# mLSTM attention and a top-1 mixture of experts in one kernel: list scatters without mutual waits, the last two items routed together, the first expert as 256 + 256 rows

## The chip, the cores and the metric

The kernel runs on one core of a Trainium2 chip. The metric is the device time of one launch in microseconds; lower is better. The numbers of the profile come from one execution that the hardware profiler recorded, the numbers of the runs from separate executions without it.

## The reference

An mLSTM recurrence over 4 batches, 8 heads, 768 tokens and a head width of 40 gives rows of 320 values for 3072 tokens; a mixture of 8 experts with top-1 routing follows. Cut to what matters:

```python
for t in range(S):                                   # per batch and head
    m_new = np.maximum(f_gate[:, :, t] + m, i_gate[:, :, t])
    f_stab, i_stab = np.exp(f_gate[:, :, t] + m - m_new), np.exp(i_gate[:, :, t] - m_new)
    C = f_stab * C + i_stab * np.einsum('bhd,bhe->bhde', vt, kt)
    n = f_stab * n + i_stab * kt
    denom = np.maximum(np.abs(nq), 1.0)              # nq = n . q
    y[:, :, t] = sigmoid(o_gate) * (C @ qt) / denom
x = y.transpose(0, 2, 1, 3).reshape(3072, 320)
logits = x @ w_gate
expert_idx = np.argmax(logits, axis=1)
gate_w = softmax(logits)[np.arange(N), expert_idx]
for e in range(8):
    xe = x[expert_idx == e]
    out[expert_idx == e] = gate_w * (np.maximum(xe @ w1[e], 0) @ w2[e])   # w1 320x1024, w2 1024x320
```

All is fp32. The experts' products run as fp32r in three parts each: an operand is split into a high part and a low part (its rest), and high x high, high x low and low x high are added.

## The kernel before

**Attention.** The recurrence is computed in chunks of 128 tokens: 6 chunks x 4 batches make 24 items (`NITEM`), taken one after the other. Step s of the loop does the score products of item s (`scores`, PE L282, DVE L292), the value products of item s-1 (`attend`, PE L309, DVE L326, then L346, which also gives the routing logits) and the end of item s-2 (`finish`, L350 to L368: the divisor, the output rows `xs`, the logits `lg`). A decay mask `dd` for each item is made by ACT and cut by GpSimd (L254); GpSimd also scales queries (`qg`, L269) and keys (`kw`, L272). PE reads `qbd` (queries by head), DMA brings it; `gb` is the item's gate row for `qg`. The finished rows go to `x_dram` (`store`, L371).

**Routing.** Groups of items (`GROUPS`: four times 4, three times 2, then item 22 and item 23 alone) go through `choose` (L377 to L395: maximum, one-hot `oh`, running counts `ohs`), `weights_of` (L399, an exponential on ACT), `count` (L401, three small matmuls for the places) and `place` (L409 to L424: the gate weight into `rec`, the place in the expert's list into `slot`, last the CAST L424). `scatter(it)` (L426) is an indirect DMA, issued by GpSimd, that writes the 128 records of an item to their places in `lst` in DRAM; one or two scatters are issued in each step. All scatters write the same DRAM tensor.

**Experts.** Expert 0 in order of size, called the first, takes its tokens of items 0 to 17 (at most HEAD = 384) as unit "a", and its late ones as unit "b" of 128 rows. A unit is read by `load_list` (L503, the list's rows by SP) and `gather` (L506, an indirect DMA for each tile of 128 rows, GpSimd), transposed on PE by thirds (`third`: L526, ACT L527, DVE L529), multiplied by w1 in eight slices f (`first`: PE L541 8 matmuls a slice, ACT L550 `hh`, DVE L551 `hl`) and by w2 for each tile of 128 rows j (`second`: PE L564 24 matmuls a tile, ACT L568, scattered to the output L569). `first` runs a few slices ahead of the hh and hl of its own slices, and calls a function in each slice; for unit a this is `last(f)`, which holds the routing of items 22 and 23. After unit a's `second` come unit b's thirds (inside the last tile), `first` and `second` of b, and then expert 1 with four tiles, 512 rows.

**Weights.** An expert's weights come in 7 chunks (`fetch`, `pull`: w1 in three of 512 KB, w2 in four of 320 KB, four raw buffers) on SP's queue; each chunk is split by ACT (high, L499) and DVE (low, L500) in `split`. The first expert's chunks are loaded in steps 14 to 20; three are split in the steps of `SPLITS`, 16, 18 and 20, (L739 and L765), the other four in slices 2, 3, 5 and 7 of unit a's `first`.

**Order.** The body is written out by hand under a manual schedule: each engine's instructions stand in the order of the code, and the framework adds the waits that the data need. On SP the loads, stores, list reads and weights share one queue in that order.

## Time and profile before

| | |
|---|---|
| Runs | 449.1, 445.7 and 447.39 us; median 447.39 us |
| Span of the profiled execution | 448.4 us |
| PE (matmul) busy | 388.3 us, 87% |
| DVE busy | 264.6 us, 59% |
| ACT busy | 195.1 us, 44% |
| GpSimd (POOL) busy | 153.4 us, 34% |
| Read from and written to DRAM | 57.97 and 8.78 MB |

PE is the engine with the most work, but the span has stretches of different kinds: attention fills it up to about 206 us, the first expert runs from 206.04 to 255.89 us, and the others after that. A busy share over the whole span says little about one stretch, so the rows below are of short windows and of single instructions. In the rows of a timeline the start, the duration, the engine, the line and operation, output and input stand in that order, and in brackets the idle time of that engine ahead of the instruction and what ended it. PE is busy while a matmul is in flight, and two overlap, so the price of one matmul is the distance between two starts and not its duration.

### The profile page before, as it was taken

The page shows a single profiled execution, that of the slowest core. Times are in us where ns is not written, and L with a number is a line of the kernel's source. Part 1 is how long each engine was busy: PE and PEld are TensorE (multiplying, and loading weights), DVE is VectorE, ACT ScalarE, POOL GpSimd, SP SyncE. Part 2 cuts the span into 40 slices and gives each one's busy share as a digit, 9 for nine tenths or more (in the row PEclk, how much of TensorE's full clock was granted, in tenths as well). Part 3 has the DMA queues.
Part 4 walks back from the last instruction along what each step waited for, and adds up shares of the span by engine and source line. Part 5 has one row for each costly group of instructions (what it writes and reads, how often), then busy time and mean ns, then how long its engine had stood idle before and what let it go on. Part 6 is the DMA issues. An engine that isn't in the chain of part 4 may idle for free. (4 is left out here: it accounts for less than half of the span.)

```text
span 448.4 us, 7609 instructions
## 1 busy us (share of the span) xinstructions
PE 388.3 (87%) x2489; PEld 350.2 (78%) x2489; DVE 264.6 (59%) x737; ACT 195.1 (44%) x438; POOL 153.4 (34%) x166
## 2 busy tenths in 40 slices
PE   7868969969968859669959999999999999979970
PEld 3657858859856738459959989889999999979970
DVE  6477978968958848478823254384572737364300
ACT  3747545526357254102623245263353646454310
POOL 5433536555643443362161031321402222221020
PEclk8989998989989879979975699999999999999995
DMA  8987685887988788521483335435445464651000
GB/s 192 235 203 188 191 213 144 190 205 178 199 217 216 183 213 186 148 69 36 95 238 103 112 103 165 118 110 168 131 146 160 109 205 131 198 157 33 12 22 11
DMA packets 42572, 66.47 MB, mean 148 GB/s; under 512 B 9232, under 2 KB 30876, under 8 KB 42516
## 3 DMA queue, kind: packets, MB, share of 16 engines
q1 hardware_dynamic: 38668, 57.35, 49.7%
q0 software_dynamic: 3456, 8.36, 6.0%
q8 instruction: 20, 0.33, 0.3%
q10 hardware_dynamic: 408, 0.27, 0.3%
q14 instruction: 20, 0.16, 0.1%
HBM read 57.97 MB, written 8.78 MB: 149 GB/s over the span
## 5 line engine op out<-in xcount | busy, mean ns | idle before, releaser
L282 PE MATMUL bank<-qbd,tq 120*128 120x384 f32 x144 | 58.6, 553 | 30.2 <-DMA qbd<-in_qk 22.1
L564 PE MATMUL bank<-w2h,hh 128*128 128x320 f32 (+1 forms) x224 | 71.8, 321 | 0.0
L551 DVE SCALAR_TENSOR_TENSOR hl<-bank,hh 128x384 fp32r<-128x384 f32 (+4 forms) x72 | 39.4, 550 | 52.3 <-ACT hh L550 51.8
L564 PE MATMUL bank<-w2l,hh 128*128 128x320 f32 (+1 forms) x224 | 70.1, 313 | 0.0
L564 PE MATMUL bank<-w2h,hl 128*128 128x320 f32 (+1 forms) x224 | 70.1, 313 | 0.0
L282 PEld LDWEIGHTS bank<-qbd,tq 120*128 120x128 f32 x144 | 30.5, 226 | 49.6 <-issue 16.3
L541 PE MATMUL bank<-xh,w1h 128*128 128x384 f32 (+3 forms) x192 | 67.2, 352 | 0.0
L541 PE MATMUL bank<-xh,w1l 128*128 128x384 f32 (+3 forms) x192 | 67.0, 350 | 0.0
L569 POOL DMA_INDIRECT out<-y,ls x24 | 23.6, 982 | 120.1 <-ACT y L568 113.2
L250 ACT ACTIVATE dd<-bank,aT 128x128 f32<-128x128 f32 x192 | 52.1, 382 | 20.2 <-PE bank L238 13.4
L292 DVE TENSOR_TENSOR pp<-bank,dd 128x384 f32<-128x384 f32 (+1 forms) x72 | 34.1, 508 | 39.5 <-PE bank L282 28.8
L550 ACT ACTIVATE hh<-bank 128x384 fp32r<-128x384 f32 (+4 forms) x72 | 35.1, 488 | 51.2 <-PE bank L541 49.3
L309 PE MATMUL bank<-pp,vz 128*123 128x128 f32 x384 | 53.1, 274 | 0.0
L309 PEld LDWEIGHTS bank<-pp,vz 128*123 128x123 f32 x384 | 47.6, 187 | 0.0
L541 PE MATMUL bank<-xl,w1h 128*128 128x384 f32 (+3 forms) x128 | 44.7, 350 | 0.0
L564 PEld LDWEIGHTS bank<-w2h,hh 128*128 128x128 f32 (+1 forms) x224 | 42.0, 188 | 0.0
L564 PEld LDWEIGHTS bank<-w2l,hh 128*128 128x128 f32 (+1 forms) x224 | 41.9, 187 | 0.0
L564 PEld LDWEIGHTS bank<-w2h,hl 128*128 128x128 f32 (+1 forms) x224 | 41.8, 187 | 0.0
L427 POOL DMA_INDIRECT lst<-rec,slot x24 | 25.0, 1043 | 43.2 <-DMA lst<-rec,slot 23.0
L269 POOL TENSOR_TENSOR qg<-tq,gb 120x384 f32<-120x384 f32 x20 | 21.2, 1059 | 53.2 <-DMA gb<-g_dram 26.8
L541 PEld LDWEIGHTS bank<-xh,w1h 128*128 128x128 f32 x192 | 36.1, 188 | 2.8 <-DVE hl L551 0.2
L541 PEld LDWEIGHTS bank<-xh,w1l 128*128 128x128 f32 x192 | 36.1, 188 | 2.5
(164 smaller groups left out, 690.7 us busy)
## 6 DMA issues: line engine op xcount, KB each, us to landing
raw<-in_w SPq DMA_DIRECT2D x32, 320.0 KB
tq<-in_qk SPq DMA_DIRECT2D x24, 360.0 KB
tk<-in_kv SPq DMA_DIRECT2D x24, 344.5 KB
raw<-in_w SPq DMA_DIRECT2D x16, 512.0 KB
sg<-in_og SPq DMA_DIRECT2D x6, 720.0 KB
raw<-in_w SPq DMA_DIRECT2D x16, 256.0 KB
x_dram<-xs SPq DMA_DIRECT2D x24, 160.0 KB
gb<-g_dram SPq DMA_DIRECT2D x20, 180.0 KB
```

Of the source, the lines that this page charges most:

```text
L250: nc.scalar.activation(dd[:, h, :], bc_ps[h // 4][:, h % 4], AF.Exp, bias=aT[:, c, i : i + 1], scale=-1.0)
L269: nc.gpsimd.tensor_mul(qg, t["tq"][:, 1], t["gb"])
L282: nc.tensor.matmul(s_ps[g][:, : n * P].rearrange("p (j t) -> p j t", j=n), t["tq"][:, 0, g, :], qbd[it % 3][:, g, :n, :], start=True, stop ...
L292: nc.vector.tensor_mul(_of(pp, g), s_ps[g][:, : n * P].rearrange("p (j t) -> p j t", j=n), _of(t["dd"], g))
L309: nc.tensor.matmul(hT, vz[it % 3][:, g, j * HW_ : (j + 1) * HW_], t["pp"][:, NG * j + g, :], start=(c == 0 and j == 0), stop=(j == n - 1),)
L427: nc.gpsimd.indirect_dma_start(out=lst, out_offset=bass.IndirectOffsetOnAxis(ap=slot[:, it : it + 1], axis=0), in_=rec[:, it, :], in_offse ...
L541: nc.tensor.matmul(ph[:, :n], a[:, k, fs], b[:, k, :n], start=not last and i == 0, stop=last and i == 2)
L550: nc.scalar.activation(hh[:, f, :n], ph[f][:, :n], AF.Relu)
L551: nc.vector.scalar_tensor_tensor(hl[:, f, :n], ph[f][:, :n], 0.0, f32(hh[:, f, :n]), ALU.max, ALU.subtract)
L564: nc.tensor.matmul(py[:T], a[:, f, ts], b[:, f], start=(f == 0 and i == 0), stop=(f == NF - 1 and i == 2))
L569: nc.gpsimd.indirect_dma_start(out=out, out_offset=bass.IndirectOffsetOnAxis(ap=ls[:T, j, 1:2].bitcast(I32), axis=0), in_=y[:T], in_offset ...
```

## The change

1. **Scatters.** They are declared to have no dependence among each other (their rows are disjoint); a one-element `memset` of a `spacer` tile precedes each. `load_list` gets a dependence on every scatter so far.
2. **Items 22 and 23** are one group of two. `finish(23)` comes ahead of unit a's `first`, with the logits ahead of the rows; the gate weights (`share`) are made in slice 0, the places, both scatters and the reads of unit b's list in slice 2.
3. **The first expert** is 256 rows in unit a (`HT` = 2 tiles) and 256 rows in unit b.
4. **Weights.** All 7 chunks of the first expert are split in steps 16 to 22 of attention. The register of expert 1 is read, and its first four chunks (512, 512, 512 and 320 KB) are loaded, at the end of the last step; its splits take the places that the first expert's had in unit a's `first`, and two tiles and three slices after. The registers of experts 2 to 7 are read after unit b's list.
5. **Start.** Of nine 512-column matmuls on zeros two stay; 24 small fp32 ones on tiles of the array follow.

```diff
-HEAD = 3 * P
+HT = 2
+HEAD = HT * P
-    i0 + n - 1: (i0, n) for i0, n in ((0, 4), (4, 4), (8, 4), (12, 4), (16, 2), (18, 2), (20, 2), (22, 1), (23, 1))
+    i0 + n - 1: (i0, n) for i0, n in ((0, 4), (4, 4), (8, 4), (12, 4), (16, 2), (18, 2), (20, 2), (22, 2))
...
-    def finish(it):
+    def finish(it, late=False):
...
+        if not late:
+            yield rows()
...
         yield nc.vector.tensor_reduce(lg[:, it, :], pl.rearrange("p g j e -> p e (g j)"), axis=AX.X, op=ALU.add)
+        if late:
+            yield rows()
...
+    scattered = []
+
     def scatter(it):
-        nc.gpsimd.indirect_dma_start(
+        nc.gpsimd.memset(spacer, 0.0)
+        ins = nc.gpsimd.indirect_dma_start(
             out=lst, out_offset=bass.IndirectOffsetOnAxis(ap=slot[:, it : it + 1], axis=0),
             in_=rec[:, it, :], in_offset=None,
         )
+        for other in scattered:
+            tc.declare_no_dep(ins.ins, other.ins, reason="disjoint rows")
+        scattered.append(ins)
...
     def load_list(ls, row, J, T):
-        nc.sync.dma_start(ls[:T, :J], lst[ds(row, T * J)].rearrange("(p j) w -> p j w", j=J))
+        ins = nc.sync.dma_start(ls[:T, :J], lst[ds(row, T * J)].rearrange("(p j) w -> p j w", j=J))
+        landed = mybir.DependencyInfo(mybir.DependencyClass.Sync, mybir.DependencyReason.DATA)
+        for other in scattered:
+            tc.add_manual_dep(ins.ins, other.ins.name, landed, reason="every scatter so far has landed")
...
+    def stir_tiles():
+        z = busy.bitcast(F32)
+        for a in (0, 64) * 4:
+            nc.tensor.matmul(bank[a // 64][:, :P], z[a : a + D, :P], z[a : a + D, :P], start=True, stop=True)
+        for a in (0, 64) * 4:
+            nc.tensor.matmul(bank[2][a : a + D + 1, :P], z[:, : D + 1], z[:, :P], start=True, stop=True)
...
-        stir(9)
+        stir(2)
+        stir_tiles()
...
-    SPLITS = (FIRST + 4, FIRST + 6, FIRST + 8)
+    SPLITS = range(FIRST + 4, NITEM - 1)
...
-            load_list(ls0, es[0] * SS, 3, P)
+            load_list(ls0, es[0] * SS, HT, P)
...
-            if chunks:
+            if s == NITEM:
+                expert(1)
+                sets[1] = {}
+                fetch(es[1], sets[1])
+                pull()
+            elif chunks:
                 pull(1)
...
         third(2)
-        weave(choose(NITEM - 2, 1))
-        weights_of(NITEM - 2, 1)
         store(NITEM - 2)
-        for r in range(1, E):
-            expert(r)
-        fetch(es[1], sets[1])
-        pull()
+        weave(finish(NITEM - 1, late=True))
+        weave(choose(NITEM - 2, 2))
+        weights_of(NITEM - 2, 2)
+        store(NITEM - 1)
         xs = {}
 
         def last(f):
             if f == 0:
-                weave(finish(NITEM - 1))
-                store(NITEM - 1)
-            if f == 1:
-                count(NITEM - 2, 1)
-                weave(place(NITEM - 2, 1), choose(NITEM - 1, 1))
+                weave(share(NITEM - 2, 2))
+            if f == 2:
+                count(NITEM - 2, 2)
+                weave(place(NITEM - 2, 2))
                 scatter(NITEM - 2)
-                weights_of(NITEM - 1, 1)
-            if f == 4:
-                count(NITEM - 1, 1)
-                weave(place(NITEM - 1, 1))
                 scatter(NITEM - 1)
-                xs["b"] = take("b", es[0] * SS + HEAD, 1, P)
+                xs["b"] = take("b", es[0] * SS + HEAD, 4 - HT, P)
+                for r in range(2, E):
+                    expert(r)
                 xs[1] = take(1, es[1] * SS, *CAPS[1])
-            if f in (2, 3, 5, 7):
+            if f in (5, 7):
                 split()
 
         first("a", sets[0], xh0, xl0, HEAD, last)
-        xt, third = transpose_x("b", xs["b"][1], 1, P)
+        xt, third = transpose_x("b", xs["b"][1], 4 - HT, P)
...
-        second("a", sets[0], ls0, 3, P, lambda j: split(), ahead)
+        second("a", sets[0], ls0, HT, P, lambda j: split(), ahead)
...
         def inner(f):
-            if f % 2:
+            if f in (1, 3, 5):
                 split()
-            if f in (1, 3, 5):
                 third1(f // 2)
```

Three places show how the instructions stand now. The first is GpSimd at the end of attention, before: `dd`, `qg` and the last scatters of attention up to the gathers of unit a (the waits in brackets are semaphores; DMASW ones are of GpSimd's own transfers, Pool of its own earlier instructions).

```order
L427 DMA lst<-rec,slot 28672x3 [waits DMASW5_49]
L254 AFFINE_SELECT dd_1910<-dd_1910 128x1024 [waits Activation_49]
L427 DMA lst<-rec,slot 28672x3 [waits DMASW6_49]
L269 TENSOR_TENSOR qg_1945<-tq_1750,gb_1840 120x384 [waits DMAHW0_49,DMAHW1_49,PE_49,Pool_49]
L427 DMA lst<-rec,slot 28672x3 [waits DMASW7_49,DVE_49]
L254 AFFINE_SELECT dd_2007<-dd_2007 128x1024 [waits Activation_49]
L427 DMA lst<-rec,slot 28672x3 [waits DMASW0_49]
L269 TENSOR_TENSOR qg_2034<-tq_1842,gb_1930 120x384 [waits DMAHW0_49,DMAHW1_49,PE_49,Pool_49]
L254 AFFINE_SELECT dd_2086<-dd_2086 128x1024 [waits Activation_49]
L269 TENSOR_TENSOR qg_2108<-tq_1932,gb_2024 120x384 [waits DMAHW0_49,DMAHW1_49,PE_49,Pool_49]
L508 DMA xg_101<-x_dram,ls_100 128x320 [waits DMAHW4_49,DMAHW5_49,DMAHW3_49,DMAHW2_49]
L508 DMA xg_101<-x_dram,ls_100 128x320 x2
```

And in the changed kernel, where L443 and L444 are the memset and the scatter, L256 is the mask, L271 `qg` and L537 the gather.

```order
L444 DMA lst<-rec,slot 28672x3 [waits DMASW7_49]
L271 TENSOR_TENSOR qg_1983<-tq_1782,gb_1874 120x384 [waits DMAHW1_49,DMAHW0_49,PE_49]
L443 MEMSET spacer 1x1 [waits Pool_49]
L444 DMA lst<-rec,slot 28672x3 [waits DMASW0_49,DVE_49]
L256 AFFINE_SELECT dd_2046<-dd_2046 128x1024 [waits Activation_49]
L443 MEMSET spacer 1x1 [waits Pool_49]
L444 DMA lst<-rec,slot 28672x3 [waits DMASW1_49]
L271 TENSOR_TENSOR qg_2075<-tq_1876,gb_1968 120x384 [waits DMAHW1_49,DMAHW0_49,PE_49]
L256 AFFINE_SELECT dd_2128<-dd_2128 128x1024 [waits Activation_49]
L271 TENSOR_TENSOR qg_2151<-tq_1970,gb_2064 120x384 [waits DMAHW1_49,DMAHW0_49,PE_49]
L537 DMA xg_102<-x_dram,ls_101 128x320 [waits DMAHW4_49,DMAHW3_49,DMAHW5_49,DMAHW2_49,DMASW2_49]
L537 DMA xg_102<-x_dram,ls_101 128x320 [waits DMASW3_49]
```

The order of the work is the same. The waits of `qg` for earlier GpSimd work are gone, each scatter has a memset ahead of it, and a scatter waits for the one eight indirect transfers before, whose semaphore it takes, in place of the one just ahead.

The second is DVE in unit a's `first`, before, where item 23 is routed: L413 to L415 make the gate weight, L420 to L424 the place, with the first expert's splits (L500) and the low parts `hl` of slices around them.

```order
L500 TENSOR_TENSOR w2l_1388<-raw_1742,w2h_1387 128x640 [waits Activation_49]
L551 SCALAR_TENSOR_TENSOR hl<-bank_132,hh 128x384 [waits Activation_49]
L500 TENSOR_TENSOR w2l_1388<-raw_1834,w2h_1387 128x640 [waits Activation_49]
L551 SCALAR_TENSOR_TENSOR hl<-bank_133,hh 128x384 [waits Activation_49]
L413 TENSOR_REDUCE es_2451<-ex_2408 128x1
L414 TENSOR_SCALAR es_2451<-es_2451 128x1 [waits DVE_49]
L415 RECIPROCAL rec<-es_2451 128x1 [waits DVE_49]
L420 TENSOR_TENSOR sl_2455<-bank_137,bump 128x8 [waits PE_49]
L421 TENSOR_TENSOR sl_2455<-sl_2455,oh 128x8 [waits DVE_49]
L423 TENSOR_REDUCE ss_2458<-sl_2455 128x1 [waits DVE_49]
L424 CAST slot<-ss_2458 128x1 [waits DVE_49]
L551 SCALAR_TENSOR_TENSOR hl<-bank_134,hh 128x384 [waits Activation_49]
```

And in the changed kernel, from the end of `choose` for both items to the places of both.

```order
L403 TENSOR_TENSOR oh<-sc_2354,m_2356 128x16 [waits DVE_49]
L405 TENSOR_TENSOR ohs<-ohs,oh 128x8 [waits DVE_49] x2
L580 SCALAR_TENSOR_TENSOR hl<-bank_133,hh 128x256 [waits DMAHW5_49,DMAHW6_49,DMAHW2_49,DMAHW7_49,DMAHW0_49,Activation_49]
L422 TENSOR_REDUCE es_2379<-ex_2361 128x2
L423 TENSOR_SCALAR es_2379<-es_2379 128x2 [waits DVE_49]
L424 RECIPROCAL rec<-es_2379 128x2 [waits DVE_49]
L580 SCALAR_TENSOR_TENSOR hl<-bank_134,hh 128x256 [waits Activation_49]
L580 SCALAR_TENSOR_TENSOR hl<-bank_135,hh 128x256 [waits Activation_49]
L433 TENSOR_TENSOR sl_2401<-bank_138,bump 128x16 [waits PE_49]
L434 TENSOR_TENSOR sl_2401<-sl_2401,oh 128x16 [waits DVE_49]
L436 TENSOR_REDUCE ss_2404<-sl_2401 128x2 [waits DVE_49]
L437 CAST slot<-ss_2404 128x2 [waits DVE_49]
```

The places of both items (the CAST, L437) stand behind the third `hl`, and no split of weights is ahead of them; before, item 23's stood behind the sixth `hl` and two splits.

The third is SP behind attention, before: the last register reads, the store of item 23 (`xs_2373`), two chunks of expert 1 and the list of unit b.

```order
L464 ISA x2
L464 TENSOR_LOAD er
L464 ISA x2
L371 DMA x_dram<-xs_2373 128x320 [waits DMAHW6_49,DVE_49]
L493 ISA
L493 DMA raw_2422<-in_w 128x1024 [waits DMAHW7_49,DVE_49]
L493 ISA
L493 DMA raw_2436<-in_w 128x1024 [waits DMAHW0_49,DVE_49]
L504 ISA
L504 DMA lsb<-lst 128x3 [waits DMASW2_49,DMAHW1_49,PE_49,Pool_49]
```

And in the changed kernel, where the stores are those of items 22 and 23 and the weights are those of expert 1.

```order
L511 ISA
L511 DMA raw_2314<-in_w 128x1024 [waits DMAHW6_49,Activation_49]
L511 ISA
L511 DMA raw_2316<-in_w 64x1024 [waits DMAHW7_49,Activation_49]
L511 ISA
L511 DMA raw_2316<-in_w 64x1024 [waits DMAHW0_49]
L511 ISA
L511 DMA raw_2319<-in_w 128x2x320 [waits DMAHW1_49,Activation_49]
L381 DMA x_dram<-xs_2281 128x320 [waits DMAHW2_49,DVE_49]
L381 DMA x_dram<-xs_2345 128x320 [waits DMAHW3_49,DVE_49]
L530 ISA
L530 DMA lsb<-lst 128x6 [waits DMASW4_49,DMASW5_49,DMASW1_49,DMASW6_49,DMASW0_49,DMASW7_49,PE_49,DMAHW4_49,Activation_49,Pool_49]
```

The chunks of expert 1 stand ahead of the stores of items 22 and 23 now (four chunks, five transfers, of which the first is not in these rows), and the list of unit b has twice the rows and waits for more transfers.

## Rows read from the trace of the kernel before

**Rows 1.** The page's slices: the span in 40 slices of 11.2 us, the mean busy share of the DMA engines in tenths.

```profile
DMA  8987685887988788521483335435445464651000
```

**Rows 2.** Windows of core 0: the window and its length in us, busy time (and instructions) of PE, PE's weight loads, DVE, ACT and POOL, then the granted clock as a share of full speed, the DMA engines' busy share and GB/s.

```profile
180.00:190.00 10.00, 5.97 (x39) 4.64 (x39) 4.03 (x14) 1.27 (x5) 3.19 (x4) 0.96 0.53 149
190.00:200.00 10.00, 6.50 (x24) 4.87 (x24) 8.77 (x26) 0.00 (x0) 6.52 (x7) 0.70 0.15 38
240.00:250.00 10.00, 10.00 (x50) 9.89 (x49) 5.27 (x11) 3.63 (x10) 0.98 (x1) 0.50 0.38 121
```

**Rows 3.** Waits from 155 to 235 us, of PE and of POOL: who waited at which line, for what, then the total in us, the number of waits and the longest.

```profile
PE bank L282 <- DMA qbd<-in_qk: 5.4, 1, 5.4
PE bank L526 <- DMA xgb<-x_dram,lsb: 4.9, 1, 4.9
POOL lst L427 <- DMA lst<-rec,slot: 18.7, 6, 5.2
```

**Rows 4.** Timeline of POOL at the end of attention.

```profile
179.11 0.97 POOL L427 DMA_INDIRECT lst<-rec,slot  x1 [3.56 <-DMA lst<-rec,slot]
186.28 1.00 POOL L427 DMA_INDIRECT lst<-rec,slot  x1 [5.16 <-DMA lst<-rec,slot]
187.31 1.10 POOL L254 TENSOR_SCALAR_AFFINE_SELECT dd<-dd 128x1024 f32<-128x1024 f32 x1
190.44 0.97 POOL L427 DMA_INDIRECT lst<-rec,slot  x1 [2.03 <-DMA lst<-rec,slot]
192.39 1.09 POOL L254 TENSOR_SCALAR_AFFINE_SELECT dd<-dd 128x1024 f32<-128x1024 f32 x1
196.84 1.01 POOL L508 DMA_INDIRECT xg<-x_dram,ls  x1 [2.41 <-DMA ls<-lst]
```

**Rows 5.** Timeline of DVE and of PE in the same stretch: the masking of scores, and the two PE instructions behind the longest idle times.

```profile
188.44 1.35 DVE L292 TENSOR_TENSOR pp<-bank,dd 128x384 f32<-128x384 f32 x3 [5.79 <-POOL dd L254]
189.05 3.64 PE L282 MATMUL bank<-qbd,tq 120*128 120x384 f32 x6 [2.73 <-DVE pp L292]
196.20 1.84 PE L346 MATMUL bank<-cs,yT 123*128 123x147 f32 x6 [3.50 <-DVE yT L326]
```

**Rows 6.** Timeline of PE at the end of attention: six of unit a's nine transposes, and its first product.

```profile
205.46 0.82 PE L526 MATMUL bank<-cs,xg 128*128 128x128 f32 x6
206.04 0.42 PE L541 MATMUL bank<-xh,w1h 128*128 128x384 f32 x1
```

**Rows 7.** The chain of unit b: the places of items 22 and 23 (DVE), their scatters and the gather of unit b (POOL), the list's read (SP).

```profile
213.08 0.15 DVE L424 CAST slot<-ss 128x1 int32<-128x1 f32 x1
214.68 0.96 POOL L427 DMA_INDIRECT lst<-rec,slot  x1 [2.74 <-DVE w2l L500]
217.13 0.15 DVE L424 CAST slot<-ss 128x1 int32<-128x1 f32 x1
220.03 0.99 POOL L427 DMA_INDIRECT lst<-rec,slot  x1 [4.39 <-DVE hl L551]
223.42 0.33 SPq L504 DMA_DIRECT2D lsb<-lst  x1
226.81 0.98 POOL L508 DMA_INDIRECT xgb<-x_dram,lsb  x1 [5.79 <-issue]
```

**Rows 8.** Transfers by issue: from issue to landing in us, the least, the median and the most of all scatters (the source line L427), then the other gathers with their median, and the gather of unit b.

```profile
DMA to landing us min/median/max: 2.5/5.6/9.4
xg<-x_dram,ls POOLq DMA_INDIRECT x27, 2.9
xgb<-x_dram,lsb POOLq DMA_INDIRECT x1, 5.8
```

**Rows 9.** Timeline of GpSimd and DVE at 230 us: a gather's issue beside the low part of a weight chunk.

```profile
230.45 1.23 DVE L500 TENSOR_TENSOR w1l<-raw,w1h 128x1024 fp32r<-128x1024 f32 x1 [5.86 <-ACT w1h L499]
230.61 1.88 POOL L508 DMA_INDIRECT xg<-x_dram,ls  x1 [0.30 <-issue]
```

**Rows 10.** Timeline of PE: the first and the 66th product of unit a's second stage; then the start of unit b (transposes), two neighbouring 128-column products, the first product of its second stage, the product of that stage at which the distance of starts went from 0.25 to 0.14 us, and the start of expert 1.

```profile
218.02 0.31 PE L564 MATMUL bank<-w2h,hh 128*128 128x320 f32 x1
227.55 0.30 PE L564 MATMUL bank<-w2h,hl 128*128 128x320 f32 x1
232.75 0.87 PE L526 MATMUL bank<-cs,xgb 128*128 128x128 f32 x3 [4.89 <-DMA xgb<-x_dram,lsb]
235.34 0.41 PE L541 MATMUL bank<-xlb,w1h 128*128 128x128 f32 x1
235.55 0.41 PE L541 MATMUL bank<-xhb,w1l 128*128 128x128 f32 x1
250.84 0.57 PE L564 MATMUL bank<-w2h,hh 128*128 128x320 f32 x1
254.13 0.31 PE L564 MATMUL bank<-w2h,hh 128*128 128x320 f32 x1
255.89 0.40 PE L541 MATMUL bank<-xh,w1h 128*128 128x512 f32 x1
```

**Rows 11.** The window around unit b's gathers, in the columns of the other windows.

```profile
228.00:230.00 2.00, 0.00 (x0) 0.00 (x0) 0.00 (x0) 0.63 (x1) 1.60 (x2) 1.00 1.02 272
```

**Rows 12.** Timeline of PE at the start: the zeros' products and the second item's scores.

```profile
1.26 3.90 PE L636 MATMUL bank<-busy 128*128 128x512 bf16 x9 [1.26 <-DVE busy L643]
19.02 1.96 PE L282 MATMUL bank<-qbd,tq 120*128 120x384 f32 x6 [2.19 <-DMA qbd<-in_qk]
```

More of the change, by code (lines that the diff above doesn't have):

```diff
@@ L407, in count, with share @@
         nc.tensor.matmul(pos, ones, baseb[:, :n], start=False, stop=True)
-    def place(i0, n):
-        o3 = oh[:, i0 : i0 + n, :]
-        pos = rt.pop(("pos", i0))
+    def share(i0, n):
         es = sm.tile([P, n], F32, name=f"es{i0}", tag="es")
@@ L415, in place @@
         yield nc.vector.reciprocal(rec[:, i0 : i0 + n, 2], es)
+    def place(i0, n):
+        o3 = oh[:, i0 : i0 + n, :]
+        pos = rt.pop(("pos", i0))
         sl = sm.tile([P, n, E], F32, name=f"sl{i0}", tag="sl")
@@ L698, in routing @@
         i0, n = GROUPS[s - 3]
+        yield from share(i0, n)
         yield from place(i0, n)
@@ L738, in step @@
         if s in SPLITS:
-            nc.scalar.copy(loaded[0][1], loaded[0][0])
+            high(loaded[0])
         if ok(s + 1):
@@ L763, in step @@
         if s in SPLITS:
-            t, h, l = loaded.pop(0)
-            nc.vector.tensor_sub(l, t, f32(h))
+            low(loaded.pop(0))
         if s == 2:
@@ L798, in step @@
         if s == EARLY + 4:
-            gather(xg0, ls0, 3, P, EARLY)
+            gather(xg0, ls0, HT, P, EARLY)
             scatter(todo.pop(0))
```

59 lines of the change are left out of this document (35 added, 24 removed).

## The prediction

> **What bounds the kernel now.** I read the page's slices first, then windows, then the waits inside them. Up to about 165 us the DMA engines are 0.7 to 0.9 busy in nearly every slice, and PE's largest wait in the stretch from 155 to 235 us that names a load is one of 5.4 us for `qbd` [rows 1, 3]: attention runs at the pace of its loads up to there. Those loads keep their order and their bytes, so I leave that part as it is; the four weight splits that it takes on more run on ACT and DVE behind such waits.
>
> From 180 to 206 us it is another limit. PE works 5.97 of 10 us and then 6.50 of 10, while the DMA share falls to 0.53 and 0.15 [rows 2]. The reader should look at who is waited for: DVE waits 5.79 us for the mask `dd`, so PE stands 2.73 us ahead of the next scores and 3.50 us for `yT` later [rows 5]. `dd` is late because GpSimd stood 5.16 us in front of a scatter, waiting for the landing of the one before; the mask starts 0.03 us after that scatter's issue ends [rows 4]. Six such waits cost GpSimd 18.7 us [rows 3]. The last of these scatters leaves at 190.44, and the list and the gathers of unit a (196.84) stand behind it [rows 4]. Then unit a's first product starts at 206.04 [rows 6]; I call this T0.
>
> Behind unit a PE has one wait of 4.89 us, for unit b's rows [rows 3, 10]. It ends a chain: place of item 23 at 217.13, scatter at 220.03, list at 223.42, gather at 226.81, landing 5.8 us later [rows 7, 8]. Then comes a stretch at the lower clock (1.2 GHz): 0.50 granted from 240 to 250 us with PE busy throughout [rows 2], and it rises where the second stage's products go from 0.27 us apart to 0.15, at 254.13 [rows 10]. From 255.89 on nothing is changed but the splits' places, so I make the sum of three terms: T0, the chain of b from T0, and the time from b's rows to expert 1.
>
> **T0.** Without the mutual waits a scatter costs GpSimd about its issue, 1.0 us [rows 4]; the added memset is one element and I put it at 0.1 us. The 5.16 us ahead of the scatter at 186.28 go, so `dd` for the next item is ready before PE asks, and PE's idle 2.73 + 3.50 = 6.2 us can go. What is late next is the load of the last item's `qbd` (PE is done with the scores before at 189.05 - 2.73 = 186.3, so it can gain only if that is there) and GpSimd's own order: the gathers still stand behind `qg` of item 23. If the last masks and `qg` move up by the same 6 us, the gathers leave at about 190.5 in place of 196.84. One tile less is transposed ahead of T0: three of nine, at 0.82 us for six [rows 6], 0.4 us and a shorter copy, together 0.6. The clock was 0.70 over 6.50 busy us [rows 2]; at full speed these would be about 1.9 us shorter, and I take half, 0.9. Against this, 1.86 MB of expert 1's weights now start at about 191, beside those gathers. No row has that pair; gathers land in 2.9 us in the median and in 5.8 for b's [rows 8], and I take off 0.7, a quarter of the difference. Sum 6.2 + 0.6 + 0.9 - 0.7 = **7.0 us**; bounds 4 (one of the two PE waits stays) and 11 (the other idle time of 180 to 190 us, 4.0 - 2.7, and the whole of the clock go too).
>
> **The chain of b.** Before, item 22's place ended at 213.23, T0 + 7.2 [rows 7], with the end of item 23 already ahead of it on DVE; the merged group does about the same instructions for two items, so I put both places at T0 + 7.4, where item 23's ended at T0 + 11.2. From place to scatter's start is 214.68 - 213.23 = 1.45 us where no scatter is waited for, and 220.03 - 217.28 = 2.75 where one is [rows 7]. So the scatters start at T0 + 8.9 and T0 + 10.1, the list is read 3.4 us after the second and the gathers start 3.4 us after that [rows 7], at T0 + 16.9 and, one issue on, 18.2. Landing takes 5.8 in the one row for b, with four other gathers issued behind it; for two tiles I take 4.3 (half way to the 2.9 of the others): T0 + 22.5. Before it was 232.75, T0 + 26.7 [rows 10]. That is 4.2. Off this comes what expert 1's splits do to GpSimd's issues: beside the low part of a chunk on DVE (1.23 us) a gather's issue took 1.88 us, against 0.98 for the one at 226.81 [rows 7, 9]. Those splits now lie around the scatters and gathers, so I take off 1.0: **3.2 us**; bounds 0 (all four issues held, and the landing as before) and 7.
>
> The Trainium skill, page "SBUF — State Buffer", section "SBUF: two separate sides", speaks against the change here: it says that GpSimd can't write the descriptors of its own transfers while DVE runs an operation that takes both ports of the pair. The row at 230.61 agrees, with 0.9 us more. By the page each of four issues could be held for one such operation, and the chain would gain 4.2 - 4 x 0.9 = 0.6 in place of 3.2; I count on one.
>
> PE's wait for b does not go: unit a's products are over sooner (128 rows fewer), so PE reaches b's transposes earlier and stands longer. This costs nothing by itself, but it is idle time ahead of a stretch whose clock is in question.
>
> **From b's rows to expert 1.** Before: 232.75 to 255.89, 23.1 us [rows 10]. It held 128-column products 0.21 us apart at the low clock, and a second stage of 24. After, at 2.4 GHz (the upper level): six transposes and the last six products of unit a 2.0 us; 64 products of 256 columns, which I scale from the 320-column ones, (227.55 - 218.02) / 65 = 0.147 us [rows 10], to 0.117, so 7.5 us (bounds 0.107, half of the 0.21 us pair, and 0.147); expert 1's thirds, 12 transposes by the row of six, 1.8; 48 second-stage products at 0.147, 7.0. Together 18.3. Of the lower clock I count a stretch as long as it lasted in the second stage before, 254.13 - 250.84 = 3.3 us [rows 10], which costs half of itself, 1.7: 20.0 us. Gain **3.1 us**; bounds 5 and -5.5.
>
> **What costs nothing.** The start: the zeros' products end at 5.2 us, and PE waits 2.19 us for a load ahead of the second item's scores [rows 12]. No row has the small fp32 ones; if they ran one after the other at the low clock to some 6 us longer, 4 us at most would show behind that wait, and if they raise the clock sooner something comes back. I take zero and keep -4 for the range. The first expert's early splits are covered by waits as above. Expert 2 to 7's register reads stand behind b's list, and what they hold up (expert 1's list) is needed only at its thirds.
>
> **Sum.** 7.0 + 3.2 + 3.1 = 13.3; 448.4 - 13.3 = 435.1 against the profiled span. The median of the runs stands 1.0 below that span, so **434.1 us**.
>
> **The rivals.**
> *Collisions:* the scatters land later in company, and unit a's gathers fall among the weights. For it: scatters took up to 9.4 us to land even one at a time [rows 8]. T0 gains 4.0, the chain nothing: 434.1 + 3.0 + 3.2 = 440.3.
> *The clock:* it stays at 1.2 GHz through all of b's first stage, and 3.3 us into the second, as it did before with PE busy throughout [rows 2, 10]. Then the stage is 3.3 + 64 x 0.21 + 12 x 0.27 + 3.3 for the first twelve and 36 x 0.147 for the other second-stage products, 28.6, which is 8.6 more than in the sum: 442.7. Against it: behind PE's idle 2.73 and 3.50 us in attention the mean clock of the window was 0.70 and not 0.50, so it came back inside that window [rows 2, 5].
> *More:* T0 gains 11, the chain 5, the rest 5, since PE's other small waits in attention go too: 447.4 - 21 = 426.4.
> *Slower:* the 1.86 MB ahead of the stores and of b's list on SP's queue. They leave at 191 and the list is wanted at T0 + 13.5 = 212.5, so the list is late if they move at under 1.86 MB / 21.5 us = 87 GB/s; to eat 13.3 us and lose 4.5 more they must move at under 47. At that point the time is 452. Against it: 272 GB/s where such loads ran with gathers [rows 11]. The Trainium skill, page "DMA: Bandwidth & Descriptors", section "Queues, rings and completion order", has each DMA engine take turns between queues; by that rule GpSimd's transfers would not stand behind all of the weights, and no row here shows the pair.
>
> **How the numbers follow.** The forecast 0.55 (its own range 428 to 439, from the bounds of the terms taken one at a time), collisions 0.18, the clock 0.13, more 0.08, slower 0.06. The range 426 to 443 leaves out the slower case and the ends of the others, which is less than 2 in 10. About 1% is what a measurement can tell from no change: 443 and 452. The clock case lies at that edge, so I give half of it and a part of the collisions (both at once make 449) to "within 1%": faster 0.82, same 0.12, slower 0.06.
>
> **What the profile after would show.** Right: no wait of `lst` on a scatter's landing at GpSimd, `dd` waited for by DVE for under 1 us in the last two items, unit a's first product at about 199; item 23's scatter 10 us after it, b's transposes 22.5 us after it, expert 1 about 20 us after those. Wrong: PE idle ahead of unit a for its gathers (collisions); a granted clock near 0.5 (1.2 GHz) through b's first stage; the list of b issued late behind weights; or the span's first 165 us longer, which none of my terms has.

## The result, and the profile after

| | before | after |
|---|---|---|
| Median of four executions | 448.25 us (445.7 to 450.38) | 433.99 us (432.93 to 435.76) |
| Ratio | | 0.968 (95% interval 0.963 to 0.974) |
| Span of the profiled execution | 448.4 us | 432.1 us |
| Unit a's first product, T0 | 206.04 us | 197.78 us |
| T0 to item 23's scatter | 14.0 us | 8.6 us |
| T0 to unit b's rows (last tile) | 26.7 us | 20.7 us |
| b's rows to expert 1 | 23.1 us | 20.2 us |
| Expert 1 to the end | 192.5 us | 193.4 us |

The forecast was 434.1. By stages the span fell by 8.3 + 6.0 + 2.9 - 0.9 = 16.3 us, where the forecast had 7.0 + 3.2 + 3.1 = 13.3. On other chips each execution of the kernel before took either 438 to 444 us, at a mean granted clock of 0.939 to 0.948, or 447 to 453 us, at 0.914 to 0.929 (the profile shown ahead has 0.924), so a ratio to it depends on which of its executions are compared (the changed kernel came to 434.71 us on one such chip, 0.986 of the shorter kind beside it, interval 0.977 to 0.994), and the experiments are read by stages first.

The timeline of POOL of the changed kernel, with the columns of [rows 4]; the same stretch:

```profile
176.49 1.10 POOL L256 TENSOR_SCALAR_AFFINE_SELECT dd<-dd 128x1024 f32<-128x1024 f32 x1
177.53 0.09 POOL L443 MEMSET spacer<- 1x1 f32 x1
177.79 0.98 POOL L444 DMA_INDIRECT lst<-rec,slot  x1 [0.17 <-issue]
182.00 1.00 POOL L271 TENSOR_TENSOR qg<-tq,gb 120x384 f32<-120x384 f32 x1 [3.24 <-issue]
182.95 1.09 POOL L256 TENSOR_SCALAR_AFFINE_SELECT dd<-dd 128x1024 f32<-128x1024 f32 x1
188.34 1.00 POOL L271 TENSOR_TENSOR qg<-tq,gb 120x384 f32<-120x384 f32 x1 [4.30 <-DMA x_dram<-xs]
189.63 1.01 POOL L537 DMA_INDIRECT xg<-x_dram,ls  x1 [0.29 <-issue]
190.95 0.96 POOL L537 DMA_INDIRECT xg<-x_dram,ls  x1 [0.30 <-issue]
```

The scatter has no wait in front of it but the 0.17 us after its memset. The mask of item 22, cut at 187.31 before, is cut at 176.49, that of item 23 at 182.95 for 192.39, and the gathers leave at 189.63 where they left at 196.84 [rows 4]. PE's side, in the timeline of PE:

```profile
185.89 1.96 PE L284 MATMUL bank<-qbd,tq 120*128 120x384 f32 x6 [0.95 <-DMA qbd<-in_qk]
195.58 0.33 PE L555 MATMUL bank<-cs,xg 128*128 128x128 f32 x1 [2.03 <-DMA xg<-x_dram,ls]
197.78 0.36 PE L570 MATMUL bank<-xh,w1h 128*128 128x256 f32 x1
```

The waits of 2.73 and 3.50 us [rows 5] are gone. What is late next is `qbd` (0.95 us) and then, as the forecast's deduction had it, unit a's second gather, which landed beside expert 1's weights and held PE for 2.03 us (with that load moved away, in experiments 5 and 7, this wait is 0.21 and 0.31 us). The windows of [rows 2] say the same: PE 8.42 and 7.90 us busy of 10, and 0.87 of the DMA engines in use where 0.15 were.

```profile
180.00:190.00 10.00, 8.42 (x62) 7.14 (x61) 9.11 (x34) 1.12 (x2) 3.40 (x4) 1.00 0.39 123
190.00:200.00 10.00, 7.90 (x67) 7.35 (x66) 5.98 (x29) 1.22 (x4) 4.78 (x8) 1.00 0.87 248
```

The chain of unit b, with the columns of [rows 7], in order of time: the place of both items (DVE), their scatters, the list (SP), and DVE's low part of a chunk beside the gathers.

```profile
204.71 0.17 DVE L437 CAST slot<-ss 128x2 int32<-128x2 f32 x1
205.16 0.95 POOL L444 DMA_INDIRECT lst<-rec,slot  x1 [3.82 <-DVE slot L437]
206.42 0.96 POOL L444 DMA_INDIRECT lst<-rec,slot  x1 [0.23 <-issue]
210.52 0.34 SPq L530 DMA_DIRECT2D lsb<-lst  x1
212.78 0.83 DVE L520 TENSOR_TENSOR w2l<-raw,w2h 128x640 fp32r<-128x640 f32 x1 [0.97 <-ACT w2h L516]
213.04 1.43 POOL L537 DMA_INDIRECT xgb<-x_dram,lsb  x1 [5.66 <-ACT w2h L516]
214.77 0.96 POOL L537 DMA_INDIRECT xgb<-x_dram,lsb  x1 [0.30 <-issue]
```

Place to scatter is 0.28 us (205.16 - 204.88); the scatters follow each other by 1.26 us, not 5.35 [rows 7]. The list's read at 210.52 waits for the second scatter, which landed 3.8 us after its issue. Then PE, in the timeline of PE from b's first transposed tile to expert 1:

```profile
216.51 0.30 PE L555 MATMUL bank<-cs,xgb 128*128 128x128 f32 x1 [2.31 <-DMA xgb<-x_dram,lsb]
218.46 1.33 PE L555 MATMUL bank<-cs,xgb 128*128 128x128 f32 x5 [1.65 <-DMA xgb<-x_dram,lsb]
221.18 0.41 PE L570 MATMUL bank<-xhb,w1h 128*128 128x256 f32 x1
221.39 0.42 PE L570 MATMUL bank<-xhb,w1l 128*128 128x256 f32 x1
221.81 0.28 PE L570 MATMUL bank<-xhb,w1l 128*128 128x256 f32 x1
221.93 0.28 PE L570 MATMUL bank<-xhb,w1h 128*128 128x256 f32 x1
238.70 0.40 PE L570 MATMUL bank<-xh,w1h 128*128 128x512 f32 x1
```

PE waits twice, 2.31 and 1.65 us, and goes on at 1.2 GHz (0.21 us from product to product) up to the third 256-column product; from then on they are 0.117 us apart. The 256-column product costs at 2.4 GHz what the forecast scaled it to.

### The profile page after: what moved, and what is told of

Read it like the earlier page. It is cut to its first block, busy times and chain, and to the rows that moved or that the text cites. A ratio compares the mean times of both kernels' runs of the same rounds, so it can differ in the third digit from the quotient of the medians.

```text
span 432.1 us, 7692 instructions
## 1 busy us (share of the span) xinstructions
PE 379.6 (88%) x2526; PEld 343.9 (80%) x2527; DVE 264.2 (61%) x725; ACT 194.5 (45%) x437; POOL 152.0 (35%) x190
## 5 line engine op out<-in xcount | busy, mean ns | idle before, releaser
L284 PE MATMUL bank<-qbd,tq 120*128 120x384 f32 x144 | 54.0, 518 | 23.2 <-DMA qbd<-in_qk 20.5
L580 DVE SCALAR_TENSOR_TENSOR hl<-bank,hh 128x256 fp32r<-128x256 f32 (+4 forms) x72 | 39.2, 550 | 50.0 <-ACT hh L579 49.3
L570 PE MATMUL bank<-xh,w1h 128*128 128x512 f32 (+4 forms) x192 | 65.2, 344 | 0.6 <-DVE hl L580 0.5
L570 PE MATMUL bank<-xh,w1l 128*128 128x512 f32 (+4 forms) x192 | 65.2, 344 | 0.0
L252 ACT ACTIVATE dd<-bank,aT 128x128 f32<-128x128 f32 x192 | 52.1, 384 | 21.3 <-PE bank L240 20.8
L284 PEld LDWEIGHTS bank<-qbd,tq 120*128 120x128 f32 x144 | 28.4, 211 | 40.4 <-issue 12.9
L579 ACT ACTIVATE hh<-bank 128x256 fp32r<-128x256 f32 (+4 forms) x72 | 35.0, 488 | 45.8 <-PE bank L570 43.7
L311 PEld LDWEIGHTS bank<-pp,vz 128*123 128x123 f32 x384 | 48.5, 190 | 0.5 <-issue 0.5
L294 DVE TENSOR_TENSOR pp<-bank,dd 128x384 f32<-128x384 f32 (+1 forms) x72 | 34.0, 507 | 23.6 <-PE bank L284 20.5
L271 POOL TENSOR_TENSOR qg<-tq,gb 120x384 f32<-120x384 f32 x20 | 20.1, 1005 | 72.6 <-DMA gb<-g_dram 18.5
L570 PE MATMUL bank<-xl,w1h 128*128 128x336 f32 (+4 forms) x128 | 43.9, 343 | 0.0
L597 ACT ACTIVATE y<-bank,ls 128x320 f32<-128x320 f32 (+1 forms) x24 | 12.7, 528 | 58.1 <-issue 46.8
```

What stands on the lines that cost most here:

```text
L252: nc.scalar.activation(dd[:, h, :], bc_ps[h // 4][:, h % 4], AF.Exp, bias=aT[:, c, i : i + 1], scale=-1.0)
L271: nc.gpsimd.tensor_mul(qg, t["tq"][:, 1], t["gb"])
L284: nc.tensor.matmul(s_ps[g][:, : n * P].rearrange("p (j t) -> p j t", j=n), t["tq"][:, 0, g, :], qbd[it % 3][:, g, :n, :], start=True, stop ...
L294: nc.vector.tensor_mul(_of(pp, g), s_ps[g][:, : n * P].rearrange("p (j t) -> p j t", j=n), _of(t["dd"], g))
L311: nc.tensor.matmul(hT, vz[it % 3][:, g, j * HW_ : (j + 1) * HW_], t["pp"][:, NG * j + g, :], start=(c == 0 and j == 0), stop=(j == n - 1),)
L570: nc.tensor.matmul(ph[:, :n], a[:, k, fs], b[:, k, :n], start=not last and i == 0, stop=last and i == 2)
```

## Experiments

The theories: **S**, the waits among scatters set T0, and the chain of scatters sets unit b's rows; **W**, the gain comes from the weights' new places; **C** and **C2**, the clock in unit b's stage decides. The stages that each profile gave, in the terms of the forecast (us; the last column is the number of unit b's rows):

| Kernel | runs, median (range) | T0 | T0 to b's rows | b's rows to expert 1 | rows of b |
|---|---|---|---|---|---|
| before (profile shown ahead) | 448.25 (445.7 to 450.4) | 206.0 | 26.7 | 23.1 | 128 |
| after | 433.99 (432.9 to 435.8) | 197.8 | 20.7 | 20.2 | 256 |
| after again | 434.71 (432.6 to 435.5) | 198.9 | 19.6 | 22.6 | 256 |
| scatters only | 434.81 (431.3 to 441.4) | 198.7 | 25.0 | 14.5 | 128 |
| waits back | 446.00 (442.6 to 454.0) | 206.8 | 24.8 | 22.2 | 256 |
| 256 + 256 only | 446.38 (444.5 to 448.4) | 206.0 | 26.6 | 20.1 | 256 |
| after, 384 + 128 | 445.34 (443.0 to 445.7) | 205.7 | 22.0 | 22.4 | 128 |
| after, weights late | 435.63 (432.7 to 438.0) | 197.8 | 23.0 | 20.5 | 256 |
| scatters only, filled | 435.29 (434.1 to 438.1) | 197.9 | 25.9 | 13.2 | 128 |
| before, filled | 451.30 (443.2 to 453.6) | 205.7 | 27.5 | 22.7 | 128 |
| after, 384 + 128, weights midway | 439.23 (438.2 to 441.7) | 198.0 | 23.1 | 24.0 | 128 |
| after, weights midway | 434.93 (434.2 to 437.8) | 197.2 | 21.4 | 20.8 | 256 |
| after, place in slice 4 | 436.53 (435.0 to 439.0) | 201.9 | 21.1 | 21.3 | 256 |
| after, old start | 435.93 (433.0 to 438.5) | 197.5 | 20.1 | 19.9 | 256 |

**1. Scatters only.** The kernel before, with part 1 alone.

```diff
+        nc.gpsimd.memset(spacer, 0.0)
+        ins = nc.gpsimd.indirect_dma_start(
...
+        for other in scattered:
+            tc.declare_no_dep(ins.ins, other.ins, reason="disjoint rows")
```

> The kernel before with the scatters' mutual waits taken away (part 1 alone): spacer memsets, no dependence among scatters, lists wait for all scatters. Theory S (these waits hold the masks and queries at the end of attention): GpSimd has no wait of lst on a scatter's landing, unit a's first product starts at 199 to 201 us instead of 206.0, and item 23's scatter, which no longer waits for item 22's, leaves about 1.3 us earlier after T0; time about 0.983 of before (441). Rival W (the waits were covered, and the change gains by its moved weight splits and loads): first product within 1.5 us of 206, time within 1% of before.

T0 198.71, and 434.8 us in the median: S. Part 1 alone brings T0's gain to within 0.9 us, and its median is that of the whole change. Item 23's scatter left 2.1 us earlier after T0 (11.9 for 14.0). Its best two runs, 431.3 (mean clock 0.95), are below all of the changed kernel's, and its worst, 438 and 441 (0.939 and 0.933), above them. PE of this kernel, unit a's first product and unit b, in timeline and windows:

```profile
198.71 0.42 PE L551 MATMUL bank<-xh,w1h 128*128 128x384 f32 x1
223.74 0.87 PE L536 MATMUL bank<-cs,xgb 128*128 128x128 f32 x3 [2.85 <-DMA xgb<-x_dram,lsb]
226.34 0.41 PE L551 MATMUL bank<-xlb,w1h 128*128 128x128 f32 x1
226.55 0.39 PE L551 MATMUL bank<-xhb,w1l 128*128 128x128 f32 x1
227.11 0.27 PE L551 MATMUL bank<-xhb,w1l 128*128 128x128 f32 x1
227.22 0.28 PE L551 MATMUL bank<-xhb,w1h 128*128 128x128 f32 x1
229.00:232.00 3.00, 3.00 (x30) 3.00 (x28) 2.42 (x5) 2.32 (x7) 0.70 (x2) 1.00 0.39 97
```

Its 128-column products begin 0.21 us apart, and after four of them they are 0.11 apart: the clock came back to 2.4 GHz and stayed, and b's stage took 14.5 us where [rows 10] had 23.1.

**2. Waits back.** The changed kernel with the scatters' mutual waits left in; the memsets and the lists' dependence on all scatters stay.

```diff
-        for other in scattered:
-            tc.declare_no_dep(ins.ins, other.ins, reason="disjoint rows")
```

> The changed kernel with the dependences among the scatters left in (part 1 alone undone, everything else as changed). Theory S: unit a's first product goes from 197.8 back to 203 to 206 us and item 23's scatter stands some 4 us behind item 22's; time 441 to 443, about 0.987 of before. Rival W: first product stays within 1.5 us of 197.8 and the time stays at 434 to 436, 0.97 of before.

T0 206.8 and 446 us, more than S said, since the chain of b is 4 us longer too (item 23's scatter 14.1 us after T0). W is out: all of the weights' new places together keep nothing of T0's gain. Beside the executions of the kernel before of 439 to 444 us this kernel is 1.0% slower (interval 0.5 to 1.5%): without part 1, the other parts cost time. Unit a's first product, in the timeline of PE, and the waits of this kernel from 155 to 235 us, to be laid beside [rows 3]:

```profile
206.76 0.36 PE L568 MATMUL bank<-xh,w1h 128*128 128x256 f32 x1
POOL lst L444 <- DMA lst<-rec,slot: 27.7, 9, 5.1
PE bank L348 <- DVE yT L328: 7.8, 2, 5.5
PE bank L553 <- DMA xgb<-x_dram,lsb: 7.9, 2, 6.6
```

**3. 256 + 256 only.** The kernel before with part 3 alone.

```diff
-HEAD = 3 * P
+HT = 2
+HEAD = HT * P
...
```

> The kernel before with the first expert as 256 + 256 rows (part 3 alone; the routing of items 22 and 23, the scatters and the place of the weights as before, with the one split that falls out of unit a's second stage done in slice 6 of unit b). Theory S: unit a's first product about 0.6 us earlier, b's rows still about 26 us after it, since the chain of scatters sets them, and PE waits longer there; from b's rows to expert 1 about 20 us at 2.4 GHz for 23.1: gain 3 to 4 us, 0.992 of before. Rival C (the clock stays at 1.2 GHz through unit b's first stage): this stretch takes 28, time 3 to 5 us more than before, 1.01.

The stages are near S's: T0 206.0 (the 0.6 did not show), b's rows 26.6 us after it for about 26, 20.1 us from there for about 20. Of the gain in time nothing is to be seen: 446.4 us is 1.5% more (interval 0.6 to 2.3%) than the executions of the kernel before of 439 to 444 us beside it, and less only than those of 447 to 450. The time is thus rival C's, though the stage is not. PE's wait for b's rows, in its timeline, is twice as long as in [rows 10], so the shorter unit a became idle time, as the forecast said of it:

```profile
232.58 1.70 PE L527 MATMUL bank<-cs,xgb 128*128 128x128 f32 x6 [9.98 <-DMA xgb<-x_dram,lsb]
```

**4. 384 + 128 in the changed kernel.**

```diff
-HT = 2
+HT = 3
...
```

> The changed kernel with the first expert as 384 + 128 rows (part 3 alone undone; one split fewer behind unit b's first stage, as a third tile of unit a takes it). Theory S: T0 about 0.6 us later; unit a's second stage is 24 products longer, so PE's wait for b's rows falls from 4 us to nearly nothing and the clock need not fall; the 128-column products cost 64 x 0.11 at 2.4 GHz, so the time is within 1% of the changed kernel, 432 to 437. Rival C: the 256-row halves are what keeps the clock up, and with 128-column products it stays at 1.2 GHz through b: 3 to 5 us more than the changed kernel, 437 to 440.

Neither: T0 went to 205.7, which no theory had. Attention ended 2.1 us later in this profile (PE's first transposition at 195.41 for 193.27). Then three gathers leave among expert 1's early weights, and the third, issued at 194.27, lets PE go on at 201.12, 6.9 us later; behind that wait PE is at 1.2 GHz up to T0. In unit b the clock was at 1.2 GHz too, as C said, from 234 to 249 us (POOL's and PE's timelines, and a window):

```profile
194.27 0.94 POOL L537 DMA_INDIRECT xg<-x_dram,ls  x1 [0.30 <-issue]
201.12 0.48 PE L555 MATMUL bank<-cs,xg 128*128 128x128 f32 x1 [3.00 <-DMA xg<-x_dram,ls]
238.00:241.00 3.00, 3.00 (x16) 3.00 (x15) 1.72 (x3) 0.90 (x3) 0.97 (x1) 0.50 0.38 99
```

So the early load cost the third gather more than the second; experiment 7 takes the load away. Since T0 moved as well, this run doesn't settle what 384 + 128 rows cost by themselves.

**5. The changed kernel again, and the weights late.** First the kernel itself beside the others, then with the load of expert 1 behind the stores of items 22 and 23.

> The changed kernel as it is, beside the three that follow on one chip. Its stretch from b's rows to expert 1 has the lower clock for only 3 us, in its first products, so its time should vary little: 432 to 436 here too, whatever the kernel before does.

434.7 us within 3 us: the time is as expected, the reason given for it is not. In this profile the lower clock lasted longer than 3 us: it came once in b's first products, as in the profile above, and again at 226 us, behind waits of 0.83 and 0.42 us ahead of expert 1's transposes. The stage took 22.6 us.

```profile
226.50:229.50 3.00, 3.00 (x17) 3.00 (x16) 1.12 (x2) 0.92 (x4) 1.01 (x1) 0.50 0.80 229
```

```diff
-            if s == NITEM:
-                expert(1)
-                sets[1] = {}
-                fetch(es[1], sets[1])
-                pull()
...
         store(NITEM - 1)
+        expert(1)
+        fetch(es[1], sets[1])
+        pull()
...
```

> The changed kernel with the load of expert 1's first four chunks moved from the end of the last attention step to behind the stores of items 22 and 23 (the splits stay as changed). Theory S: the load is a cost to T0 as it is placed, since unit a's second gather landed 4.6 us after its issue beside it; T0 1 to 2 us earlier (196 to 197), the chain of b unchanged or up to 1 us longer, since the weights fall nearer to its list; time 0.5 to 2 us less than the changed kernel. Rival W: the early load is a source of the gain; without it the splits in unit a's last slices wait for weights and the time rises by 3 us or more.

T0 is 1.1 us earlier than in the run beside it (197.8 for 198.9), b's rows 3.4 us later after T0, the median 0.9 us more, which the two ranges don't tell apart. PE's wait for unit a's second gather is nearly gone, but a wait for DVE stands behind it, so from PE's first transposition to T0 it is 3.8 us for 4.7:

```profile
194.47 0.33 PE L555 MATMUL bank<-cs,xg 128*128 128x128 f32 x1 [0.21 <-DMA xg<-x_dram,ls]
196.53 1.02 PE L348 MATMUL bank<-cs,yT_last 123*128 123x147 f32 x6 [0.90 <-DVE yT_last L328]
```

In b's chain the list was read 6.4 us after the last scatter's issue, for 3.7 us in the run beside it: the scatter now lands beside the weights, which leave from 202.6 to 207.1 us. So the early load costs T0 about what it was charged and saves more in b's chain; the 3 us of rival W did not show.

**6. A fill for PE's wait.** Products that nothing reads stand ahead of unit b's transposes, 12 in the kernel with the scatters alone, 18 in the kernel before.

```diff
             if j == 2:
+                for _ in range(12):
+                    nc.tensor.matmul(bank[2], mparts[:, :P], mparts[:, :512], start=True, stop=True)
                 for k in range(3):
```

> The kernel before with the scatters' mutual waits taken away and twelve products of 512 columns, whose result nothing reads, ahead of unit b's transposes (2.6 us at 2.4 GHz, inside PE's wait of 2.85). Theory C2 (what makes the kernel before and the one with the scatters alone spread over 10 us is whether the clock falls in PE's wait for b's rows, since 128-column products then stay at 1.2 GHz): the products keep it up, b's rows to expert 1 take 14.5 to 15.5 us in every run, and all runs lie within 3 us of 431. Rival N (the spread comes from loads in attention): runs still spread from 431 to 441.

> The kernel before with eighteen such products ahead of unit b's transposes (3.8 us at 2.4 GHz, inside PE's wait of 4.9), nothing else. Theory C2: b's rows to expert 1 go from 23.1 to 14.5 to 16 us, the runs that were at 446 to 450 come down to 439 to 442 and the spread is under 4 us. Rival N: median and spread as those of the kernel before.

The first did as C2 said in the stage: 13.2 us, 128-column products 0.11 us apart from the first ones on, and four runs within 4 us. But they lie at 434 to 438 and not within 3 us of 431: what came after expert 1's start took 197.0 us in the profiled run, for 190.9 to 193.8 in all others but the filled kernel before (195.4). A part of this is one wait of 1.68 us for the rows of a later expert at 361.86, behind which the clock falls; the filled kernel before has the same at 380.72 (1.91 us), the other profiles at most 0.3 us in this place. Why those rows came late is open. The second failed: PE still waited 1.84 us behind the fill, and the clock fell and stayed low through the stage; its runs, 443 to 454, are spread as N had it, so N is not out for the kernel before. The first kernel's window in b's stage, that late wait and the window behind it, then windows of the second (PE's clock is the third column from the right):

```profile
229.00:232.00 3.00, 3.00 (x30) 3.00 (x29) 2.91 (x8) 2.14 (x6) 1.53 (x1) 1.00 0.53 175
361.86 0.31 PE L536 MATMUL bank<-cs,xg 112*128 112x112 f32 x1 [1.68 <-DMA xg<-x_dram,ls]
362.00:365.00 3.00, 3.00 (x15) 3.00 (x15) 1.33 (x2) 1.06 (x2) 0.00 (x0) 0.63 0.38 107
```

```profile
235.00:238.00 3.00, 3.00 (x16) 3.00 (x16) 0.29 (x1) 0.64 (x2) 0.72 (x1) 0.50 0.43 125
244.00:247.00 3.00, 3.00 (x17) 2.89 (x16) 1.15 (x4) 0.72 (x3) 0.00 (x0) 0.50 0.58 210
```

**7. 384 + 128 once more, with the load behind the store of item 22; and the same load with 256 + 256.**

```diff
...
         store(NITEM - 2)
+        expert(1)
+        fetch(es[1], sets[1])
+        pull()
         weave(finish(NITEM - 1, late=True))
```

> The changed kernel with the first expert as 384 + 128 rows and the load of expert 1's first chunks behind the store of item 22, ahead of that of item 23, so that it starts when unit a's gathers have landed. Theory S: T0 198 to 200 (its third gather landed 6.8 us after its issue beside the early load), scatter of item 23 8.7 us after T0, PE's wait for b's rows under 1 us since unit a is longer, the clock mostly up: b's rows to expert 1 13.5 to 15 us; time 427 to 431, less than any so far. Rival C: with 128-column products the clock is at 1.2 GHz in this stretch in half the executions all the same, and the times spread over 8 us: 428 to 438.

> The changed kernel with only that load moved, behind the store of item 22. Theory S: unit a's gathers land within 3 us of their issue, T0 1 to 1.5 us earlier than with the early load (196.5 to 197.8), b's rows 20.5 to 21.5 us after T0, time 431 to 434. Rival: the load then meets the list and the gathers of unit b, as where it stood behind both stores (b's rows 23 us after T0), and time is 434 to 437.

With 384 rows T0 was back at 198.0, so the early load was what had moved most of it. But b's stage took 24.0 us: PE had no wait for b's rows, and three of 0.45 to 1.40 us for expert 1's inside the stage, and from there to 243 us the clock was low. S failed in the stage and the time, and rival C holds for the clock, if not for the spread (3.5 us): the median is 4.3 us above that of the kernel with 256 rows beside it, and its lowest run (438.2) above the other's highest (437.8). Its PE timeline and windows:

```profile
227.69 0.86 PE L555 MATMUL bank<-cs,xg 128*128 128x128 f32 x2 [1.40 <-DMA xg<-x_dram,ls]
229.00:232.00 3.00, 3.00 (x16) 3.00 (x16) 0.98 (x2) 0.49 (x3) 1.01 (x1) 0.50 0.84 202
238.00:241.00 3.00, 3.00 (x15) 3.00 (x15) 0.82 (x3) 0.56 (x2) 0.00 (x0) 0.50 0.00 0
```

With 256 rows the stages are S's (T0 197.2, b's rows 21.4 us after it), but the time, 434.9, is 0.9 us above S's range and what it was for the changed kernel on other chips: the load's place makes no difference that the runs can tell.

**8. The places in slice 4, and the old start.**

```diff
-            if f == 2:
+            if f == 4:
                 count(NITEM - 2, 2)
```

> The changed kernel with the places, scatters and list read of items 22 and 23 in slice 4 of unit a's first stage instead of slice 2. Theory S (unit b's rows come at the end of the chain place, scatter, list, gather, and PE waits for them): scatter of item 23 and b's rows 1.5 to 2 us later, expert 1 too, time 1.5 to 3 us more than the changed kernel. Rival: b's rows are late for another reason (the gathers' landing among expert 1's weights), and b's rows and the time move by under 0.5 us.

Open: after T0 the scatter left 1.4 us later than in the profile of the changed kernel and the list was read 1.2 us later, as S has it, but the second gather left 0.6 and b's rows came 0.5 us later, which is within what they vary from run to run (19.6 to 21.4). The median is 0.6 to 1.6 us above the two kernels beside it that keep slice 2. T0 in this profile is late for another reason, its attention (PE's first transposition at 196.55 for 193.27).

```diff
-        stir(2)
-        stir_tiles()
+        stir(9)
```

> The changed kernel with the nine products on zeros of the kernel before at the start (part 5 undone). Theory S: the second item's scores wait for their load in both, so nothing after 20 us moves: times within 0.7% of the changed kernel. Rival: the small products raise the clock ahead of the first scores (1.94 us for 3.36) and 1 to 2 us of the gain are theirs.

435.9 us, T0 197.5: S, the start is worth nothing that can be measured. The scores of the first item, which took 3.36 us in the profile of the kernel before, took 1.94 with the old start too, and the second item's scores waited 2.77 us for their load (timeline of PE):

```profile
7.97 1.94 PE L284 MATMUL bank<-qbd,tq 120*128 120x384 f32 x6
19.16 1.14 PE L284 MATMUL bank<-qbd,tq 120*128 120x384 f32 x2 [2.77 <-DMA qbd<-in_qk]
```

## Why the prediction held, and where its terms were off

**The span's offset.** The step "the median of the runs stands 1.0 below that span" set three executions against the span of another. The time of an execution stands above its own span: by 1.7 to 1.9 us in the changed kernel (the profiled execution is one of its four runs, 433.83 for 432.1), by 2.1 to 2.2 us in the kernel before, so that its profiled execution took about 450.5 us by this estimate and was among its slowest. The terms came to 3.0 us more than forecast, and the offset took 2.9 back: that the forecast lies 0.1 us from the median is luck. So is the gain of 14 us in part: against the executions of the kernel before of 438 to 444 us some 6 us are left, and the rest is there only against those of 446 and more.

**T0: 8.3, forecast 7.0, right in its mechanism.** Scatters only and waits back show it from both sides: 198.7 with part 1 alone, 206.8 with all but part 1. Both of PE's waits went, as the sum had it. The deduction for the weights was 0.7: from PE's first transposition of unit a to T0 it was 4.5 and 4.7 us with the early load, 3.8 and 4.0 without it (weights late and midway). T0 itself differs by 1.1 us between the two profiles of the changed kernel, so its single values say no more than that.

**The chain of b: 6.0, forecast 3.2, right in its mechanism, with three terms mis-sized.** Place to scatter was 0.28 us and not 1.45, and two landings were shorter: list to gather 2.5 for 3.4, and the second gather let PE go on after 3.7 for 4.3 (against them, scatter to list was 4.1 for 3.4). The 1.45 was called the time "where no scatter is waited for", and that reading was wrong: item 21's scatter left at 210.99 and landed 2.9 us later, at 213.9, so 0.7 of the 1.45 us were a mutual wait. In the rest a low part of a chunk ran on DVE [rows 7]; how much of it that cost is not shown. POOL's timeline and the landing of this one scatter, before:

```profile
210.99 0.96 POOL L427 DMA_INDIRECT lst<-rec,slot  x1 [1.79 <-DMA lst<-rec,slot]
lst<-rec,slot POOLq DMA_INDIRECT x1, 2.9
```

With part 1 alone it was 0.28 us too, with the same low part next on DVE (scatters only, 206.25 to 206.53). On the rule of the Trainium skill, page "SBUF — State Buffer", section "SBUF: two separate sides" (GpSimd can't write descriptors while DVE holds the pair of ports), the trace agrees with its 1.43 us gather beside a low part, for 0.96 without; it hit one of the four issues, by 0.5 us, and I had taken off 1.0. What rests on stages alone is the share of the merged routing in this; it was not run by itself.

**From b's rows to expert 1: 2.9, forecast 3.1.** The price of 0.117 us and the short stretch at 1.2 GHz are in the rows above; a wait of 0.94 us for expert 1's rows at 224.94, for which the sum had no term, was nearly balanced by small differences elsewhere. With 256 rows b's stage took 19.9 to 22.6 us in all eight profiles. What the forecast had not seen is that the 23.1 us of before were one of two cases: with 128 rows the stage took 13.2 or 14.5 us where the clock was up and 22.4 to 24.0 where it was not. So 256 + 256 costs some 6 us against the good case and saves 3 against the bad one. In the terms of the change: part 1 gives the 8 to 9 us, and its median alone (434.81) is that of the whole. Parts 2 and 3 shorten b's chain and make the stage more alike from one execution to the next, which shows in the spread (432.6 to 435.8 in eight runs, for 431.3 to 441.4 in four with part 1 alone) and not in the median; the near relatives with 256 rows spread over 5 us as well (weights late, old start).

That the spread of the kernel before has this cause was not shown on it: its filled version kept the low clock. Its granted clocks speak for it. Between the executions of 438 to 444 us and those of 447 to 453 us the mean clock differs by some 0.02, which by an estimate is 18 us more at 1.2 GHz (0.02 / 0.5 x 445 us) and up to 9 us of time; the profile of before is at 0.50 from 231 to 254 us, that of scatters only for 3 us in this stage. Where the executions without a profile had their lower clock is not shown.

**The rivals.** *Slower* did not happen: b's list was read 4.1 us after the last scatter's issue, which is the scatter's own landing and not the weights' queue. *Collisions* happened in full where three gathers met the weights; with two they cost PE a wait of 2.0 to 2.3 us, of which about 0.7 reached T0. *The clock* did not stay low with 256 columns, though it fell a second time in one of eight profiles; with 128 columns it was low through the stage in four of six, came back early in one (scatters only) and never fell in one (its filled version). **Costs at nothing:** the start was nothing; the 0.9 us that were lost behind expert 1's start are within the 191 to 194 us that this stretch takes in most profiles.

## What to carry to other kernels

In this kernel's framework, writes to disjoint rows of one DRAM tensor wait for each other unless told otherwise, and what they cost is found behind them on the issuing engine: here masks and query scaling, and through them PE. A stage whose products are short and follow a wait can run at either clock in different executions; read several profiles before pricing a change against one of them. A load moved into an idle stretch of the queues has to be checked against the small gathers that end the next chain.
